# Row tiles of 32 for the first transforms, and filter taps of two terms with the products summed by VectorE in place

## The chip, the cores and the metric

The kernel runs on one NeuronCore of a Trainium2 chip. The core has a matrix engine (TensorE, PE in the profile, with its weight loads listed apart as PEld), VectorE (DVE), ScalarE (ACT), GpSimd (POOL) and a queue engine SyncE (SP) that here issues most of the transfers. The engines run side by side, each in its own fixed order, and wait for each other on semaphores. SBUF is the working memory of 128 partitions, PSUM the small memory into which TensorE writes its sums. The metric is the device time of one execution in microseconds, a median over executions; lower is better.

## The reference, cut to what matters

Two independent halves write the left and right 576 columns of a 2048 x 1152 output. The left half is a sliding window attention (32 heads of 18, window 256) behind a projection `x @ wqkv` and in front of `@ wo`. The right half is a state space convolution of `u` (2048 x 576) with a filter that is itself computed from 128 complex states for each channel:

```
P = jnp.exp(logdA[:, :, None] * l[None, None, :])
K = jnp.einsum("dn,dnl,dn->dl", Cc, P, dB).real      # the filter taps, d = 576, l = 2048
...
Yf = Uf * Kf                                         # FFTs over 2L = 4096
y  = irfft(Yf)[:L] + u * Dskip
```

So the filter taps K, the transforms of u and of K, their product and the inverse transform are what the right half computes. The kernel does the transforms by matrix products in two steps: a first transform of length 32 over the coarse index of time, a second of length 64 with the twiddles in its matrices.

## The kernel before, in words

The program has three stretches. The order of instructions in the first two is made by a planner: the instructions are traced in program order, and a scheduler places each on its engine by the costs that it assumes and by the dependences it sees; what the engine runs is that fixed order. The third stretch is placed in the written order (`manual_schedule`, line 991).

**Projection and tables, about 0 to 428 us.** Three generators are merged (lines 972 to 974): `proj` (lines 182 to 252, the projection, whose matmuls are on line 172 and whose results are read out by L236 on ScalarE and L237 on VectorE and stored by SP on L178 to L180 and L250), `tables` (lines 430 to 456, the filter), and `s1_u` (lines 470 to 477, the first transform of u).

The filter is built in 36 half groups c of 16 channels (`HC`); two halves form one of 18 groups. The 2048 taps of a channel are written as 32 coarse times 64 fine positions. For a half group:

- `exps_ab`, `exps_q`, `factors`, `phases` (lines 333 to 375 and 389 to 391) make small tables: outer products on TensorE (L314), exponentials and sines on ScalarE (L331), the fraction of an angle on ScalarE and VectorE (L324 to L326), and complex factors on GpSimd (L362 to L373). `factors` leaves A (12 wide: minus the imaginary part, the real part, the imaginary part) and `tr` (real and imaginary).
- `products` (lines 377 to 387) lets GpSimd multiply A with the real part of `tr` into m0 and A with the imaginary part into m1, each 128 partitions x 16 channels x 64 values in f32. Both come from pool P with two buffers for each name.
- `qtable` (lines 393 to 409) lets ScalarE make a sine and a cosine in PSUM and VectorE multiply them into Q (L404 to L407).
- `taps` (lines 411 to 428) is a sum over the states on TensorE in f32. For each channel four terms are accumulated in PSUM: both 32-wide halves of m0 and of m1, against the two halves of Q. Four channels at a time use four column strips of 32 of the array. After two half groups ScalarE copies kp into K (L428).

In `tables`, `taps(c - 1)` is written ahead of `products(c + 1)`: with two buffers the products of c + 1 reuse the buffers that the taps of c - 1 have read.

**The first transforms.** `s1` (lines 459 to 468) multiplies a block of 128 partitions (4 column groups of 144 channels x 32 coarse times) by a 128 x 128 matrix with four 32 x 32 blocks on its diagonal: one for the cosine part, one for the sine part. Each part goes through a PSUM bank (pool `pps`, three banks that the projection uses too), is copied out by ScalarE or every fourth time by VectorE (`evac`, L128 and L130) into a staging tile of pool `s1s` (two buffers), and is stored to DRAM by one transfer (L468). `s1_u` does this for u in 16 blocks during the first stretch; `s1_k` (lines 479 to 483) for K in 8 blocks after the last taps, with three PSUM banks of its own.

**Convolution and attention, from about 478 us.** `conv` (lines 485 to 585) loads for each of 16 pairs of frequencies the tables and the transformed u and K (`tx`, `tk`, L493 and L496, one pair ahead), transforms, multiplies, and inverts; it is woven into the attention by hand (lines 774 to 849).

What the change and the prediction touch: `w1` (lines 44 to 47 and 955), `gx` and `gk` (957, 958), the pools on 969 and 970, `products`, `taps`, `s1`, and `load` in `conv` (490 to 497).

Of the kernel before, what the change touches and what calls it, by code (L numbers as in the profile page):

```python
# [10 lines left out]
F32 = mybir.dt.float32  # L11
# [4 lines left out]
OP = mybir.AluOpType  # L16
# [10 lines left out]
JJ2 = JJ // 2  # L27
# [11 lines left out]
def constants():  # L39
    c = {}  # L40
    tau = 2 * np.pi
    l1, l2, f1, f2 = np.arange(32), np.arange(64), np.arange(32), np.arange(64)
    ph = -tau * np.outer(l1, f1 + 0.25) / 32
    w1 = np.zeros((128, 2, 128))
    for s in range(4):
        w1[s * 32:s * 32 + 32, 0, s * 32:s * 32 + 32] = np.cos(ph)
        w1[s * 32:s * 32 + 32, 1, s * 32:s * 32 + 32] = np.sin(ph)
    w2 = np.zeros((128, 32, 128))
    i1 = np.zeros((128, 32, 128))
    for f in range(32):  # L50
        ph = -tau * np.outer(l2, f + 0.25 + 32 * f2) / 2048
        co, si = np.cos(ph), np.sin(ph)
        w2[0:64, f, 0:64], w2[64:128, f, 0:64] = co, -si
        w2[0:64, f, 64:128], w2[64:128, f, 64:128] = si, co
        i1[0:64, f, 0:64], i1[64:128, f, 0:64] = co.T, si.T
        i1[0:64, f, 64:128], i1[64:128, f, 64:128] = -si.T, co.T
    ph = tau * np.outer(f1 + 0.25, l1) / 32
# [45 lines left out]
class Kernel:  # L103
# [271 lines left out]
        yield  # L375

    def products(self, c):
        A, tr = self.AB[c // 2]
        ch = slice(c % 2 * HC, c % 2 * HC + HC)
        sh = [128, HC, 8, 8]  # L380
        r = []
        for part, a0 in ((0, 4), (1, 0)):
            m = self.p["P"].tile(sh, F32, name="m%d" % part)
            self.nc.gpsimd.tensor_tensor(m, A[:, ch, a0:a0 + 8].unsqueeze(3).to_broadcast(sh),  # L384
                                         tr[:, ch, part, 0:8].unsqueeze(2).to_broadcast(sh), op=OP.mult)
            r.append(m.rearrange("p c a b -> p c (a b)"))
        self.P[c] = r

    def phases(self, c):
        x = self.outer(self.ps, c // 2, [self.mul["c_ct"]], c % 2 * HC, HC)  # L390
# [20 lines left out]
    def taps(self, c):  # L411
        nc = self.nc
        if c % 2 == 0:
            self.kp = self.p["kps"].tile([128, JJ, 64], F32, name="kp")
        kp, Q, (m1, m2) = self.kp, self.Q.pop(c), self.P.pop(c)
        for j in range(JJ2):
            for term in range(4):
                m = (m1, m2)[term // 2]
                a0 = term % 2 * 32
                for st in range(4):  # L420
                    ch = st * JJ2 + j
                    nc.tensor.matmul(kp[32 * st:32 * st + 32, c % 2 * JJ2 + j, :], m[:, ch, a0:a0 + 32],  # L422
                                     Q[:, ch, term % 2, :], start=(term == 0), stop=(term == 3), skip_group_check=True)
            if j % 2:
                yield
        if c % 2:
            q = c // 2
            nc.scalar.activation(self.K[:, :, q * JJ:q * JJ + JJ].rearrange("p l j -> p j l"), kp, AF.Copy)  # L428
# [28 lines left out]


    def s1(self, src, g, l0, nl, pp):
        nc, n = self.nc, nl * 144  # L460
        for part in range(2):
            st = self.p["s1s"].tile([128, n], F32, name="g1")
            k = n // 2 if n <= 576 else n // 3
            for o in range(0, n, k):
                ps = self.p[pp].tile([128, 512], F32, name="pp")[:, :k]
                nc.tensor.matmul(ps, self.w1[:, part, :], src[:, o:o + k], start=True, stop=True)  # L466
                self.evac(st[:, o:o + k], ps)
            nc.sync.dma_start(g[part, l0:l0 + nl].rearrange("l p j -> p l j"), st.rearrange("p (l j) -> p l j", j=144))  # L468

    def s1_u(self):  # L470
        uv = self.a["u"].rearrange("(p l) (s j) -> s p l j", l=64, j=144)
# [13 lines left out]
    def conv(self):  # L485
        nc, a, tt = self.nc, self.a, self.nc.vector.tensor_tensor
        fs, fy = self.p["fs"], self.p["fy"]

        def load(fp):
            t = {}  # L490
            for nm, src in (("w2", a["c_w2"]), ("i1", a["c_i1"])):
                t[nm] = fs.tile([128, 2, 128], F32, name=nm)
                nc.sync.dma_start(t[nm], src[:, 2 * fp:2 * fp + 2])  # L493
            for nm, g in (("tx", self.gx), ("tk", self.gk)):
                t[nm] = fs.tile([128, 4, 2, 144], F32, name=nm)
                nc.sync.dma_start(t[nm], g.rearrange("a l (s f) j -> (a l) s f j", s=4)[:, :, 2 * fp:2 * fp + 2, :])  # L496
            return t

        def ring():
# [69 lines left out]
        for qd in range(16):  # L569
# [7 lines left out]
            for hf in range(2):  # L577
                for k in range(2):
                    nc.tensor.matmul(pair[hf][64 * k:64 * k + 64], self.i2, hp[:, k, hf * 288:hf * 288 + 288],
                                     start=True, stop=True)  # L580
# [367 lines left out]
    def build(self):  # L948
        nc, a = self.nc, self.a
        with ExitStack() as es:  # L950
            self.pool(es, "const", 1)
            self.pool(es, "dram", 1, DRAM)
            self.pool(es, "dram2", 2, DRAM)
            cp, dp = self.p["const"], self.p["dram"]
            self.w1 = cp.tile([128, 2, 128], F32, name="w1")
            nc.gpsimd.dma_start(self.w1, a["c_w1"])
            self.gx = dp.tile([2, 64, 128, 144], F32, name="gx")
            self.gk = dp.tile([2, 64, 128, 144], F32, name="gk")
            self.h = dp.tile([2, 64, 32, D], F32, name="h")
            with ExitStack() as ek:  # L960
                self.pool(ek, "K", 1)
                with ExitStack() as e1:
                    for n, b, s in (("s4c", 1, None), ("pps", 3, PSUM), ("xps", 2, PSUM), ("trig", 1, PSUM),
                                    ("kps", 1, PSUM)):
                        self.pool(e1, n, b, s)
                    with ExitStack() as e2:
                        self.pool(e2, "prep", 1)
                        self.s4_prep()
                    for n, b in (("wq", 1), ("raw", 2), ("x", 1), ("pst", 2), ("s1u", 2), ("s1s", 2), ("ab", 2), ("abt", 1), ("mab", 4),
                                 ("mg", 4), ("fr", 2), ("Q", 2), ("P", 2)):  # L970
                        self.pool(e1, n, b)
                    proj, tables, s1u = self.proj(), self.tables(), self.s1_u()
                    merge((part(proj, 16), 16), (part(tables, 20), 20), (part(s1u, 4), 4))
                    merge((proj, 56), (tables, 304), (s1u, 12))
                with ExitStack() as e1:
                    self.pool(e1, "s1s", 2)
                    self.pool(e1, "s1p", 3, PSUM)
                    for _ in self.s1_k():
                        pass
            with ExitStack() as e1:  # L980
                self.pool(e1, "fc", 1)
                self.i2 = self.p["fc"].tile([128, 64], F32, name="i2")
                nc.sync.dma_start(self.i2, a["c_i2"])
# [44 lines left out]
```

## Time and profile before

| | |
|---|---|
| Median of 3 runs | 1046.06 us (1044.16 to 1049.4) |
| Profiled execution | 1041.77 us; its span from first to last instruction 1040.1 us |
| TensorE busy (matmuls) | 842.3 us, 81% of the span |
| VectorE busy | 703.1 us, 68% |
| ScalarE busy | 569.9 us, 55% |
| GpSimd busy | 593.5 us, 57% |
| First stretch, 104 to 416 us | TensorE busy 288.67 of 312 us |
| First transform of K, 430 to 478 us | transfers at 227 GB/s, DMA engines busy 76% |

A row of a group in the profile reads: line, engine, operation, output <- inputs by the program's names, shapes, count | busy time of the group and the mean duration of one in ns | idle time of the engine just before, with what ended it. The busy time is a union: where instructions overlap it is less than count times mean, and the ratio of the two says how many were in flight together. A row of a table by stretches gives the stretch, its length, then busy time and count for each engine, the granted TensorE clock as a share of full speed, the busy share of the DMA engines and GB/s. A row of waits gives the waiting engine, tile and line, what ended the wait, the total in us, how many times and the longest. A row of the chain gives start, length and what ran or was waited for. Each f32 matmul of the program appears as two TensorE instructions in the profile (the 64 matmuls that `taps` issues for a half group are its x128).

### The profile page before, as it was taken

The page shows a single profiled execution, that of the slowest core. Times are in us where ns is not written, and L with a number is a line of the kernel's source. Part 1 is how long each engine was busy: PE and PEld are TensorE (multiplying, and loading weights), DVE is VectorE, ACT ScalarE, POOL GpSimd, SP SyncE. Part 2 cuts the span into 40 slices and gives each one's busy share as a digit, 9 for nine tenths or more (in the row PEclk, how much of TensorE's full clock was granted, in tenths as well). Part 3 has the DMA queues.
Part 4 walks back from the last instruction along what each step waited for, and adds up shares of the span by engine and source line. Part 5 has one row for each costly group of instructions (what it writes and reads, how often), then busy time and mean ns, then how long its engine had stood idle before and what let it go on. Part 6 is the DMA issues. An engine that isn't in the chain of part 4 may idle for free.

```text
span 1040.1 us, 26776 instructions
## 1 busy us (share of the span) xinstructions
PE 842.3 (81%) x10332; PEld 443.0 (43%) x10332; DVE 703.1 (68%) x1805; ACT 569.9 (55%) x883; POOL 593.5 (57%) x714
## 2 busy tenths in 40 slices
PE   1433998989799899865788888878888999987787
PEld 0212456446457457532343333333333444433345
DVE  2879374674765675464867788878878676767554
ACT  1784466666666666331266565556666565634470
POOL 0036495674676596301266776757776757664780
PEclk9956899999999999898899999999999999989999
DMA  9655544443454333587144465464544563579863
GB/s 271 182 169 154 133 108 102 113 99 84 124 114 106 79 89 92 135 257 218 48 126 136 130 209 157 147 177 129 158 124 146 144 184 113 152 175 240 222 185 124
DMA packets 155911, 152.27 MB, mean 146 GB/s; under 512 B 36856, under 2 KB 134392, under 8 KB 155592
## 3 DMA queue, kind: packets, MB, share of 16 engines
q1 hardware_dynamic: 148152, 131.98, 46.8%
q0 software_dynamic: 6128, 14.60, 5.5%
q10 hardware_dynamic: 1504, 3.99, 1.4%
q8 instruction: 81, 1.33, 0.6%
q14 instruction: 46, 0.38, 0.1%
HBM read 89.12 MB, written 61.01 MB: 144 GB/s over the span
## 4 chain that ended last, share of the span: by engine, by line
PE 40%; DVE 21%; DMA 12%; issue 10%; ACT 7%; POOL 7%; SPq 2%; DVEq 0%; ACTq 0%; POOLq 0%
PE pp L172 11%; PE r L641 4%; PE kp L422 4%; PE r L505 4%; PE po L705 4%; PE r L908 4%; DVE jk L648 3%; PE pp L466 3%; POOL P L693 3%; PE x L314 2%; DMA gk<-g 2%; PE ST L682 2%; DVE qb L632 2%; ACT P L684 2%; PE r L513 2%
## 5 line engine op out<-in xcount | busy, mean ns | idle before, releaser
L648 DVE CUSTOM_DVE_ANT_0 jk<-r,bias 128x288 f32<-128x288 f32 (+7 forms) x512 | 198.4, 433 | 96.8 <-PE r L641 95.9
L684 ACT ACTIVATE P<-ST,esc 128x1024 f32<-128x1024 f32 (+1 forms) x192 | 201.8, 1058 | 94.5 <-PE ST L682 93.5
L693 POOL TENSOR_SCALAR_AFFINE_SELECT P<-P 128x512 f32<-128x512 f32 x240 | 171.1, 741 | 107.0 <-ACT P L684 104.6
L384 POOL TENSOR_TENSOR m<-A,tr 128x1024 f32<-128x1024 f32 x72 | 145.6, 2045 | 86.8 <-PE kp L422 79.6
L641 PE MATMUL r<-K,qb 128*64 128x288 f16 (+7 forms) x1024 | 130.4, 297 | 38.3 <-DVE qb L632 11.2
L541 POOL TENSOR_TENSOR Y<-t,t 64x288 f32<-64x288 f32 x64 | 52.9, 826 | 119.8 <-DMA tk<-gk 59.8
L705 PE MATMUL po<-P,V 128*32 128x256 f32 (+2 forms) x1408 | 100.6, 397 | 16.9 <-ACT osb L713 8.1
L641 PEld LDWEIGHTS <-qb 128*64 128x64 f16 x1024 | 60.1, 109 | 121.3 <-issue 67.3
L422 PE MATMUL kp<-Q,m 128*32 128x64 f32 x4608 | 80.6, 224 | 16.5 <-issue 6.1
L422 PEld LDWEIGHTS kp<-Q,m 128*32 128x32 f32 x4608 | 70.4, 112 | 38.8 <-issue 26.6
L466 PE MATMUL pp<-ut,w 128*128 128x288 f32 x128 | 47.8, 506 | 42.6 <-DMA ut<-in_u_dram 25.4
L682 PE MATMUL ST<-Q,K 64*128 64x384 f16 (+2 forms) x704 | 73.8, 281 | 3.0 <-DMA Q<-mt 2.9
L325 DVE TENSOR_TENSOR k<-x,k 128x512 f32<-128x512 f32 (+1 forms) x54 | 33.9, 638 | 39.1 <-ACT k L324 39.0
L237 DVE SCALAR_TENSOR_TENSOR qst<-pp,qst 128x512 f16<-128x512 f32 x36 | 24.7, 685 | 50.6 <-ACT qst L236 42.4
L705 PEld LDWEIGHTS po<-P,V 128*32 128x32 f32 x1408 | 35.8, 110 | 51.4 <-issue 26.4
L542 POOL TENSOR_TENSOR Y<-t,t 64x288 f32<-64x288 f32 x64 | 54.4, 851 | 3.8
L172 PE MATMUL pp<-xh,wh 128*128 128x512 f16 x180 | 48.3, 391 | 9.4 <-DVE xh L229 6.5
L128 ACT ACTIVATE g<-pp 128x288 f32<-128x288 f32 (+1 forms) x84 | 34.1, 447 | 37.9 <-DMA gk<-g 20.0
L362 POOL TENSOR_TENSOR tr<-tr,mab 128x768 f32<-128x768 f32 x18 | 34.7, 1929 | 31.1 <-ACT tr L331 31.1
L466 PEld LDWEIGHTS pp<-ut,w 128*128 128x128 f32 x128 | 26.5, 227 | 58.2 <-ACT g L128 17.5
L172 PEld LDWEIGHTS <-wh 128*128 128x128 f16 x324 | 31.6, 99 | 45.7 <-issue 12.4
L505 PE MATMUL r<-tx,w 128*64 128x288 f32 x256 | 41.2, 439 | 10.7 <-DMA tx<-gx 9.5
(173 smaller groups left out, 1755.4 us busy)
## 6 DMA issues: line engine op xcount, KB each, us to landing
gx<-g SPq DMA_DIRECT2D x32, 288.0 KB
qd<-qst SPq DMA_DIRECT2D x72, 128.0 KB
gk<-g SPq DMA_DIRECT2D x16, 576.0 KB
tx<-gx SPq DMA_DIRECT2D x16, 576.0 KB
tk<-gk SPq DMA_DIRECT2D x16, 576.0 KB
h<-ho SPq DMA_DIRECT2D x16, 576.0 KB
raw<-in_xT_dram SPq DMA_DIRECT2D x16, 512.0 KB
Q<-qd SPq DMA_DIRECT2D x32, 216.0 KB
```

The lines of the kernel that those rows point to most:

```text
L172: self.nc.tensor.matmul(ps, u, v, start=(i == 0), stop=(i == len(ops) - 1))
L384: self.nc.gpsimd.tensor_tensor(m, A[:, ch, a0:a0 + 8].unsqueeze(3).to_broadcast(sh), tr[:, ch, part, 0:8].unsqueeze(2).to_broadcast(sh), o ...
L422: nc.tensor.matmul(kp[32 * st:32 * st + 32, c % 2 * JJ2 + j, :], m[:, ch, a0:a0 + 32], Q[:, ch, term % 2, :], start=(term == 0), stop=(ter ...
L466: nc.tensor.matmul(ps, self.w1[:, part, :], src[:, o:o + k], start=True, stop=True)
L505: nc.tensor.matmul(ps[64 * par:64 * par + 64], w2[:, par, 64 * part:64 * part + 64], t[:, 2 * hs:2 * hs + 2, par, :], start=True, stop=True)
L542: nc.gpsimd.tensor_tensor(Y[par][64:128], t1[sl, 1], t2[sl, 1], op=OP.add)
L641: nc.tensor.matmul(ps[64 * b:64 * b + 64, :n], self.qb[:, b, t, :], d["K"][:, b, k0:k0 + n], start=True, stop=True, skip_group_check=True)
L648: nc.vector.tensor_tensor_reduce(out=jk[:, :n], in0=ps[:, :n], in1=self.bias[:, 288 - n:], scale=1.0, scalar=-3e38, op0=OP.add, op1=OP.max ...
L682: nc.tensor.matmul(ps[:, u, o:o + n], d["K"][h, jp, k0:k0 + 128], d["Q"][h, jp, q0:q0 + n], start=True, stop=True, skip_group_check=True)
L684: nc.scalar.activation(pt[:, 2 * jp:2 * jp + 2, lo:hi], ps[:, :, lo:hi], AF.Exp, scale=self.esc)
L693: nc.gpsimd.affine_select(v, v, pattern=[[0, 4], [sg, 128]], compare_op=OP.is_ge, fill=0.0, base=-1 if far else 0, channel_multiplier=-sg)
L705: nc.tensor.matmul(self.po[32 * j:32 * j + 32, t0 * 128:t1 * 128], V[:, kb * 76 + 19 * j:kb * 76 + 19 * j + 32], pt[:, j, o:o + (t1 - t0) ...
```

## The change

- The matrix of the first transform becomes one 128 x 64 tile: 32 rows of cosine next to sine, repeated for the four groups of 32 partitions. `s1` issues for each piece of columns four matmuls with 32 rows and 64 columns of weights, one for each group of partitions, into the lower and upper halves of two PSUM tiles allocated together, in place of two matmuls with 128 rows and 128 columns. The number of read-outs stays. The staging tiles get two names (g0, g1) with two buffers each. Each block is stored by four transfers of 64 partitions in place of two of 128; the elements of 576 bytes stay.
- `gx` and `gk` in DRAM become [64, 4, 64, 144], and `load` fetches `tx` and `tk` by two transfers of 64 partitions each in place of one of 128.
- In `products`, VectorE adds m1 to m0 in place after GpSimd has made both. `taps` accumulates two terms in place of four. Pool P becomes P0 with two buffers for m0 and P1 with one buffer for m1.

```diff
-        w1[s * 32:s * 32 + 32, 0, s * 32:s * 32 + 32] = np.cos(ph)
-        w1[s * 32:s * 32 + 32, 1, s * 32:s * 32 + 32] = np.sin(ph)
+    w1 = np.tile(np.concatenate([np.cos(ph), np.sin(ph)], axis=1), (4, 1))
...
-            m = self.p["P"].tile(sh, F32, name="m%d" % part)
+            m = self.p["P%d" % part].tile(sh, F32, name="m%d" % part)
...
-            r.append(m.rearrange("p c a b -> p c (a b)"))
-        self.P[c] = r
+            r.append(m)
+        self.nc.vector.tensor_tensor(r[0], r[0], r[1], op=OP.add)
+        self.P[c] = r[0].rearrange("p c a b -> p c (a b)")
...
-            for term in range(4):
-                m = (m1, m2)[term // 2]
-                a0 = term % 2 * 32
+            for term in range(2):
                 for st in range(4):
                     ch = st * JJ2 + j
-                    nc.tensor.matmul(kp[32 * st:32 * st + 32, c % 2 * JJ2 + j, :], m[:, ch, a0:a0 + 32],
-                                     Q[:, ch, term % 2, :], start=(term == 0), stop=(term == 3), skip_group_check=True)
+                    nc.tensor.matmul(kp[32 * st:32 * st + 32, c % 2 * JJ2 + j, :], P[:, ch, 32 * term:32 * term + 32],
+                                     Q[:, ch, term, :], start=(term == 0), stop=(term == 1), skip_group_check=True)
...
     def s1(self, src, g, l0, nl, pp):
         nc, n = self.nc, nl * 144
-        for part in range(2):
-            st = self.p["s1s"].tile([128, n], F32, name="g1")
-            k = n // 2 if n <= 576 else n // 3
-            for o in range(0, n, k):
-                ps = self.p[pp].tile([128, 512], F32, name="pp")[:, :k]
-                nc.tensor.matmul(ps, self.w1[:, part, :], src[:, o:o + k], start=True, stop=True)
-                self.evac(st[:, o:o + k], ps)
-            nc.sync.dma_start(g[part, l0:l0 + nl].rearrange("l p j -> p l j"), st.rearrange("p (l j) -> p l j", j=144))
+        st = [self.p["s1s"].tile([128, n], F32, name="g%d" % e) for e in range(2)]
+        k = n // 2 if n <= 576 else n // 3
+        for o in range(0, n, k):
+            ps = [self.p[pp].tile([128, 512], F32, name="pp")[:, :k] for _ in range(2)]
+            for q in range(4):
+                r, h = slice(32 * q, 32 * q + 32), 64 * (q % 2)
+                nc.tensor.matmul(ps[q // 2][h:h + 64], self.w1[r], src[r, o:o + k], start=True, stop=True,
+                                 skip_group_check=True)
+            for e in range(2):
+                self.evac(st[e][:, o:o + k], ps[e])
+        for q in range(4):
+            h = 64 * (q % 2)
+            nc.sync.dma_start(g[l0:l0 + nl, q].rearrange("l p j -> p l j"),
+                              st[q // 2][h:h + 64].rearrange("p (l j) -> p l j", j=144))
...
-                nc.sync.dma_start(t[nm], g.rearrange("a l (s f) j -> (a l) s f j", s=4)[:, :, 2 * fp:2 * fp + 2, :])
+                for e in range(2):
+                    f0 = 32 * e + 2 * fp
+                    nc.sync.dma_start(t[nm][64 * e:64 * e + 64], g[:, :, f0:f0 + 2])
...
-            self.w1 = cp.tile([128, 2, 128], F32, name="w1")
+            self.w1 = cp.tile([128, 64], F32, name="w1")
...
-            self.gx = dp.tile([2, 64, 128, 144], F32, name="gx")
-            self.gk = dp.tile([2, 64, 128, 144], F32, name="gk")
+            self.gx = dp.tile([64, 4, 64, 144], F32, name="gx")
+            self.gk = dp.tile([64, 4, 64, 144], F32, name="gk")
...
-                                 ("mg", 4), ("fr", 2), ("Q", 2), ("P", 2)):
+                                 ("mg", 4), ("fr", 2), ("Q", 2), ("P0", 2), ("P1", 1)):
```

More of the change, by code (lines that the diff above doesn't have):

```diff
@@ L43, in constants @@
     ph = -tau * np.outer(l1, f1 + 0.25) / 32
-    w1 = np.zeros((128, 2, 128))
-    for s in range(4):
-        w1[s * 32:s * 32 + 32, 0, s * 32:s * 32 + 32] = np.cos(ph)
-        w1[s * 32:s * 32 + 32, 1, s * 32:s * 32 + 32] = np.sin(ph)
+    w1 = np.tile(np.concatenate([np.cos(ph), np.sin(ph)], axis=1), (4, 1))
     w2 = np.zeros((128, 32, 128))
@@ L414, in taps @@
             self.kp = self.p["kps"].tile([128, JJ, 64], F32, name="kp")
-        kp, Q, (m1, m2) = self.kp, self.Q.pop(c), self.P.pop(c)
+        kp, Q, P = self.kp, self.Q.pop(c), self.P.pop(c)
         for j in range(JJ2):
-            for term in range(4):
-                m = (m1, m2)[term // 2]
-                a0 = term % 2 * 32
+            for term in range(2):
                 for st in range(4):
                     ch = st * JJ2 + j
-                    nc.tensor.matmul(kp[32 * st:32 * st + 32, c % 2 * JJ2 + j, :], m[:, ch, a0:a0 + 32],
-                                     Q[:, ch, term % 2, :], start=(term == 0), stop=(term == 3), skip_group_check=True)
+                    nc.tensor.matmul(kp[32 * st:32 * st + 32, c % 2 * JJ2 + j, :], P[:, ch, 32 * term:32 * term + 32],
+                                     Q[:, ch, term, :], start=(term == 0), stop=(term == 1), skip_group_check=True)
             if j % 2:
```

## The prediction

> **What bounds the kernel now.** I read the busy shares of 40 slices first: TensorE is near full only from the fifth to the sixteenth slice, so I asked for the stretch in which the changed code runs, then for its chain, its waits and its groups. First the busy times by stretch (TensorE, weight loads, VectorE, ScalarE, GpSimd; clock, DMA share, GB/s):
>
> ```profile
> 104.00:416.00 312.00, 288.67 (x5147) 176.32 (x5150) 188.26 (x278) 196.98 (x351) 203.61 (x161) 0.98 0.44 104
> 416.00:430.00 14.00, 10.10 (x381) 8.56 (x371) 6.46 (x10) 4.17 (x7) 9.12 (x8) 0.89 0.45 102
> 430.00:478.00 48.00, 35.87 (x96) 17.40 (x94) 28.57 (x27) 16.13 (x36) 0.40 (x1) 0.96 0.76 227
> ```
>
> From 104 to 416 us TensorE is busy 92.5% of the time and no other engine over 66%: it is the bound there. From 430 to 478 us, the first transform of K, nothing is full but the transfers come nearest. The chain of that stage (start, length, what):
>
> ```profile
> 434.26 3.43 DMA gk<-g
> 437.79 0.50 ACT g L128
> 438.33 2.22 PE pp L466 x6
> 440.57 0.57 DVE g L130
> 441.20 5.37 DMA gk<-g
> ```
>
> It is a loop over two staging buffers: store, wait until it has landed, read out into the freed buffer, store. Next the waits of VectorE and GpSimd from 104 to 416 us:
>
> ```profile
> POOL m L384 <- PE kp L422: 79.0, 9, 14.1
> POOL tr L362 <- ACT tr L331: 21.4, 12, 4.0
> ...
> DVE qst L237 <- ACT qst L236: 42.4, 17, 5.5
> DVE k L325 <- ACT k L324: 39.0, 11, 14.2
> DVE Q L406 <- ACT sn L331: 16.6, 12, 2.7
> ```
>
> GpSimd makes products as soon as the taps free a buffer, and VectorE never waits for GpSimd. Groups with count, union and mean, from the page:
>
> ```profile
> L384 POOL TENSOR_TENSOR m<-A,tr 128x1024 f32<-128x1024 f32 x72 | 145.6, 2045 | 86.8 <-PE kp L422 79.6 <-issue 7.2
> L422 PE MATMUL kp<-Q,m 128*32 128x64 f32 x4608 | 80.6, 224 | 16.5 <-issue 6.1
> L466 PE MATMUL pp<-ut,w 128*128 128x288 f32 x128 | 47.8, 506 | 42.6 <-DMA ut<-in_u_dram 25.4
> L682 PE MATMUL ST<-Q,K 64*128 64x384 f16 (+2 forms) x704 | 73.8, 281 | 3.0 <-DMA Q<-mt 2.9
> L505 PE MATMUL r<-tx,w 128*64 128x288 f32 x256 | 41.2, 439 | 10.7 <-DMA tx<-gx 9.5
> ```
>
> Count times mean over union gives the matmuls in flight: 1.36 in L466 on the whole array, 2.7 in L505 on two column halves, 2.7 in L682 on two row halves, 12.8 in L422 on four column strips. Last, VectorE beside GpSimd (start, length):
>
> ```profile
> 301.96 1.78 DVE L326 TENSOR_SCALAR ab<-k 128x512 int32<-128x512 int32 x1
> ```
>
> This operation takes 0.34 us at best and 2.15 at worst. Here GpSimd ran products from 299.57 us, 1.99 each; the second ended near 303.55 and L326 at 303.74. The two engines exclude each other in such cases.
>
> **The change, part by part.** The sum is made against the profiled execution, 1041.77 us, span 1040.1 us; the median of the three runs is 4.3 us above it.
>
> *Taps of two terms.* Half of L422's instructions go. From 104 to 416 us they hold TensorE 67.85 us, so 33.9 us go, all on the bounding engine.
>
> *Row tiles for u.* In that stretch L466 holds TensorE 27.0 us (x88, 11 of the 16 blocks). The new form has twice the instructions, each with a quarter of the rows and half of the columns of the array. No row shows f32 in row tiles. If four run together (as four strips do in L422), 13.5 us go; if only two do (L505, L682), nothing; if none, 27 us are added. L682 shows row tiles overlapping and L422 four in flight, so I take four. TensorE needs 288.7 - 33.9 - 13.5 = 241.3 us.
>
> *The sums on VectorE.* 36 additions of 128 x 1024 f32, both inputs in SBUF. Nearest rows with two SBUF inputs: 512 elements 0.68 us at best (L764), 576 elements 0.76 us (L575). At about 1.04 ns an element plus 0.15 us one takes 1.21 us, 33 of them (65 products lie in this stretch) 40 us. L764's median is 1.12 and its longest 1.29 us, in the stretch where GpSimd works beside it. So each addition may also wait out a product that GpSimd has begun: 0 to 1.95 us; I take half, 1 us, since GpSimd pauses after many products (the 79 us of waits). VectorE: 188.3 + 40 + 33 = 261 us. GpSimd, held during the additions: 203.6 + 40 = 244 us at most.
> The Trainium skill, "SBUF — State Buffer", section "SBUF: two separate sides", says it more strongly: the pair of ports that the two engines share is an exclusive lock for a whole instruction, and a VectorE operation with two SBUF inputs takes it. L326 agrees (1.78 for 0.34 us). By that rule every addition right behind a product whose successor has started would pay the full 1.95 us.
>
> *What bounds that stretch then.* Three engines at 241 to 261 us, ScalarE at 197. With the 92.5% that TensorE reaches now the largest gives 282 us; with 90%, because three nearly equal engines wait for each other more often, 290. I take 286: 26 us less than 312. Ends: 261 us (TensorE alone bounds, additions never wait) and 316 us (all additions pay 1.95 us: 188.3 + 40 + 64 = 292 at 92.5%), that is -51 to +4. The planner will lay out a new order, which no row shows.
>
> *The new wait.* An addition at the head of VectorE's queue until its m1 is there holds back the read-outs of the projection (L237), the fractions and Q. Behind them stand TensorE (PSUM banks) and ScalarE's sines. With one buffer for m1 the next m1 waits for the addition too. In the order of before the products lay several us ahead of their taps, so I charge nothing beyond the 1 us above and make the rest a rival.
>
> *78 to 104 us.* Here VectorE is busy 23.91 of 26 us and carries the chain; two additions fall in: +2.4 us.
>
> *416 to 430 us.* The last taps run alone, L422 busy 6.1 us: half goes, -3 us (0 to -6, with the 2.5 us in which TensorE waited for its instructions).
>
> *First transform of K.* TensorE has 35.87 us in 48 and is not the bound; the buffers are, 27.3 us of read-outs waiting for `gk<-g` to land. With twice the staging the stage runs at what the transfers give: 227 GB/s x 48 us = 10.9 MB; at the 257 GB/s of its best slice 42.4 us, at the kernel's best slice (271) 40.2. I take -5.5 us (-8 to 0, should stores of 64 partitions be slower).
> The skill's page just named, section "Door 1: The DMA port swizzle", gives 64 partitions half of 436 GB/s, 218; if the halves did not overlap, 9.44 MB of stores would take 43 us, and the gain would be nearer 4 us. No row here shows it.
>
> *SP.* 22 more issues of gx at 0.38 us by 416 us, 16 more of gk, 64 more for tx and tk of at most 0.6 us. Behind them on SP stand the stores of qd; SP's waits from 104 to 416 us sum to over 140 us, which hides 9 us. The loads of tx and tk are issued a pair of frequencies ahead, and TensorE waited for tx once (9.5 us, at the start): +0.5 us there. If that cover went, each pair would pay some 0.6 us, 10 in all.
>
> Sum: -26 + 2.4 - 3 - 5.5 + 0.5 = -31.6, so 1010 for the profiled execution and 1014 against the median.
>
> **The rivals.**
> - *VectorE stands for GpSimd (slower).* The planner places the addition where the real product, at 2 us, is not done. If each waits one product and half of another, 2.9 us: (188.3 + 33 x 4.1) / 0.925 = 350 us, +38. With the other terms 1074, against the median 1079. It decides above 2.1 us a wait, where the stage grows by the 5.6 us that the other terms gain and another 5. For it: GpSimd's products start late now, behind the taps, and VectorE's order is fixed. Against it: three PSUM banks of projection work (3 us each) lie between VectorE and TensorE.
> - *VectorE becomes the bound with full waits for the ports.* Stage +4, sum -1.6: 1044, no change. For it L326; against it GpSimd's pauses.
> - *The row tiles do not overlap.* TensorE 288.7 - 33.9 + 27 = 282, at 92.5% 305 us, -7; the K stage has 72 us of matmul in place of 36, +24. Sum +17: 1063. Against it L682.
> - *TensorE stays the only bound.* -51 + 2.4 - 6 - 8 = -62.6: 984. For it: every wait of VectorE in the stretch follows TensorE's or ScalarE's work.
>
> **How the numbers follow.** Forecast 1014, chance 0.50, its own range 996 to 1034 (the stage at 94% or 85% of the largest demand, 278 to 307). TensorE alone 984: 0.14. No change 1044: 0.14. VectorE standing 1079: 0.15. Row tiles serial 1063: 0.07. Half a per cent, 5 us, is about what a measurement tells from no change. Faster: 0.50 + 0.14 + a third of the 1044 case = 0.69. Same: 0.10. Slower: 0.21. The range leaves out half of the fastest case and most of the slowest: 986 to 1062.
>
> **What would show it.** Right: L422 x2304 with half the busy time; the stretch from 104 us to the last taps about 25 us shorter; TensorE below 90% in it; the new addition near 1.2 to 2.2 us; L466 with twice the count and about half the union; hardly a wait for `gk<-g`. Wrong: long waits of VectorE for m on line 384's successor, then of ScalarE and TensorE for VectorE; L466 with a larger union; landing times of gk above 5.4 us.

## The result and the profile after

The changed kernel takes 1104.83 us in the median (1098.41 to 1110.41) against 1045.11 us for the kernel before on the same chip: 1.056 times as long, 95% interval 1.049 to 1.064. Its profiled execution took 1098.41 us, the span is 1096.7 us against 1040.1. Five marks, each the start of an instruction that both kernels have, say where the 56.6 us lie:

| mark, us from the span's start | before | after | stretch ending there |
|---|---|---|---|
| first matmul of the projection | 105.8 | 118.7 | +12.9 |
| last read-out of kp into K | 428.4 | 465.0 | +23.7 |
| last store of gk issued | 476.7 | 505.0 | -8.3 |
| first matmul on tx | 484.4 | 537.4 | +24.7 |
| end of the span | 1040.1 | 1096.7 | +3.6 |

So the filter's stretch lost 36.6 us in two pieces, the transform of K gained 8.3, and then 24.7 us were lost in a place that holds no changed instruction but the loads of tx and tk. The same three stretches as busy times of the changed kernel (TensorE, weight loads, VectorE, ScalarE, GpSimd; clock, DMA share, GB/s):

```profile
118.70:465.01 346.31, 295.80 (x3377) 153.92 (x3376) 234.66 (x318) 200.71 (x358) 213.52 (x166) 0.90 0.42 96
468.00:505.00 37.00, 28.38 (x180) 9.15 (x176) 6.69 (x12) 15.41 (x34) 0.00 (x0) 0.87 0.89 232
506.00:537.00 31.00, 0.00 (x0) 0.00 (x0) 21.67 (x16) 0.00 (x0) 3.51 (x1) 0.50 0.52 131
```

In the first row TensorE is busy 85% and VectorE 68%: nobody is full, yet the stretch is longer. The same stretch of the kernel before, from its own first projection matmul to its last read-out into K:

```profile
105.79:428.41 322.62, 298.26 (x5512) 184.37 (x5511) 191.96 (x285) 198.33 (x355) 211.14 (x168) 0.98 0.44 104
```

TensorE's busy time is 296 us in place of 298 although 39% of its instructions are gone: the granted clock is 0.90 against 0.98, and one and the same group of projection matmuls takes 440 ns in the mean against 391. In the last row of the three TensorE and ScalarE do nothing at all for 31 us while VectorE and GpSimd fill memory. The groups of the changed kernel that answer to those shown before:

```profile
L382 POOL TENSOR_TENSOR m<-A,tr 128x1024 f32<-128x1024 f32 x72 | 144.9, 2023 | 94.0 <-PE kp L419 54.0
L465 PE MATMUL pp<-ut,w 32*64 32x288 f32 x256 | 50.5, 545 | 44.9 <-DMA ut<-in_u_dram 24.3
L385 DVE TENSOR_TENSOR m<-m,m 128x1024 f32<-128x1024 f32 x36 | 48.1, 1338 | 53.2 <-POOL m L382 52.9
L419 PE MATMUL kp<-Q,m 128*32 128x64 f32 x2304 | 54.3, 239 | 26.2 <-DVE Q L406 9.8
```

L385 is the new sum: 1.34 us in the mean, less than the 2.2 us costed with the wait for the ports, but VectorE stood 52.9 us in front of it for GpSimd's product. L419 has half the instructions and two thirds of the time of L422, not half. L465, the row tiles, has 256 x 0.545 / 50.5 = 2.8 matmuls in flight against 1.36, and twice as many to do: no gain. The waits of the changed kernel from 104 to 468 us:

```profile
POOL m L382 <- PE kp L419: 54.0, 9, 9.3
PEld L169 <- issue: 50.5, 99, 4.0
DVE m L385 <- POOL m L382: 48.5, 18, 7.8
POOL m L382 <- DVE m L385: 38.5, 25, 2.8
...
ACT sn L328 <- DVE Q L406: 28.6, 10, 7.2
...
PE x L311 <- DVE k L322: 20.2, 11, 3.7
```

The two engines that did not wait for each other before now do so both ways, and TensorE's weight loads for the projection (L169) wait 50.5 us for nothing that the profile names, against 21.9 before. The taps hardly wait for the sum itself (0.8 us, once). What comes late is VectorE's other work: TensorE waits 20.2 us for the fractions (L322), against 3.4 before, and ScalarE 28.6 us for Q, against 20.9. The first of the two pieces begins ahead of the projection; from the same kernel in order of time (start, length):

```profile
83.10 2.96 DVE L385 TENSOR_TENSOR m<-m,m 128x1024 f32<-128x1024 f32 x1 [4.46 <-POOL m L382]
...
86.25 4.15 DVE L207 SCALAR_TENSOR_TENSOR wl<-K,wr,wh 128x2160 f16<-128x2160 f32 x1
...
118.70 4.96 PE L169 MATMUL pp<-xh,wh 128*128 128x512 f16 x12 [0.66 <-ACT xh L223]
```

VectorE stands 4.5 us for the first product with the splitting of the weights (L207) queued behind, which the projection needs; the sum and the split each take longer beside GpSimd (2.96 and 4.15 us against 1.21 and 2.46 at best). This is not the whole 12.9 us: with the sums alone (e3 below) VectorE stands 6.1 us at the same place, and the projection starts only 2 us later. Last, the empty stretch behind the transform of K:

```profile
509.57 3.51 POOL L603 MEMSET qb<- 128x4096 f16 x1 [47.87 <-DMA i<-in_c_i_dram]
509.65 0.30 DVE L599 MEMSET bias<- 128x288 f32 x1 [6.40 <-DMA i<-in_c_i_dram]
...
530.02 1.21 SPq L502 DMA_DIRECT2D tx<-gx  x2
...
537.42 2.19 PE L511 MATMUL r<-tx,w 128*64 128x288 f32 x8 [34.77 <-DMA tx<-gx]
```

These are the attention's set-up: memsets, and loads that SP issues in turn with them. Before, the same memsets ran from 427 to 475 us beside the transform of K. Now they start some 4.5 us after its last store was issued, and the loads of tx stand behind them on SP. The profile names a load (`i`) as what released them here; e1 has the same gap, and there it names a store of gk.

### The profile page after: what moved, and what is told of

Same layout as the page of the kernel before. It is cut to its first block, busy times and chain, and to the rows that moved or that the text cites. A ratio compares the mean times of both kernels' runs of the same rounds, so it can differ in the third digit from the quotient of the medians.

```text
span 1096.7 us, 22681 instructions
## 1 busy us (share of the span) xinstructions
PE 839.6 (77%) x8252; PEld 400.8 (37%) x8252; DVE 751.1 (68%) x1841; ACT 570.3 (52%) x883; POOL 599.5 (55%) x714
## 4 chain that ended last, share of the span: by engine, by line
PE 19%; DVE 13%; issue 6%; POOL 5%; DMA 4%; ACT 2%; SPq 1%; DVEq 0%; POOLq 0%; ACTq 0%
PE r L647 4%; PE po L711 4%; PE r L511 4%; DVE jk L654 3%; PE r L914 3%; POOL P L699 2%; PE ST L688 2%; PE r L519 2%; DVE qb L638 2%; DVE osb L770 1%; DMA out_dram<-t 1%; ACT P L690 1%; DMA X<-in_u_dram 1%; DVE m L654 1%; DVE t L542 1%
## 5 line engine op out<-in xcount | busy, mean ns | idle before, releaser
L465 PE MATMUL pp<-ut,w 32*64 32x288 f32 x256 | 50.5, 545 | 44.9 <-DMA ut<-in_u_dram 24.3
L385 DVE TENSOR_TENSOR m<-m,m 128x1024 f32<-128x1024 f32 x36 | 48.1, 1338 | 53.2 <-POOL m L382 52.9
L419 PE MATMUL kp<-Q,m 128*32 128x64 f32 x2304 | 54.3, 239 | 26.2 <-DVE Q L406 9.8
L359 POOL TENSOR_TENSOR tr<-tr,mab 128x768 f32<-128x768 f32 x18 | 38.6, 2146 | 54.0 <-ACT tr L328 47.4
L169 PE MATMUL pp<-xh,wh 128*128 128x512 f16 x180 | 56.7, 440 | 10.2 <-DVE xh L226 8.2
L419 PEld LDWEIGHTS kp<-Q,m 128*32 128x32 f32 x2304 | 41.6, 120 | 55.7 <-issue 26.3
L537 ACT ACTIVATE X<-r 128x288 f32<-128x288 f32 x64 | 25.6, 410 | 65.7 <-DMA tk<-gk 36.8
L169 PEld LDWEIGHTS <-wh 128*128 128x128 f16 x324 | 33.1, 105 | 56.2 <-issue 27.4
L169 PE MATMUL pp<-xh,wl 128*128 128x512 f16 x180 | 50.9, 410 | 0.0
L328 ACT ACTIVATE mg<-x 128x512 f32<-128x512 f32 x72 | 40.7, 599 | 13.2 <-PE x L311 12.8
```

The source lines that it names most:

```text
L169: self.nc.tensor.matmul(ps, u, v, start=(i == 0), stop=(i == len(ops) - 1))
```

## The experiments

Ratios are against runs of the kernel before beside them on the same chip (medians 1042 to 1044 us), with the 95% interval.

### The staging of K's transform

**e1, four staging buffers in the kernel before, nothing else.**

```diff
-                    self.pool(e1, "s1s", 2)
+                    self.pool(e1, "s1s", 4)
```

> The kernel before with one edit: four staging buffers in place of two for the first transform of K alone. Theory L (layout): doubling that staging, as the change does by its two names, makes it reach the addresses of the attention's set-up tiles, so that the set-up (memsets of VectorE and the loads of the first units, about 20 us) can start only when the last store of K's transform has landed. Then: the stage some 5 to 7 us shorter, the stretch from its last store to the first matmul on tx some 25 us longer, in all 1060 to 1068 against 1045. Rival S (stores): the late set-up comes from the four stores of 64 partitions, which are not here. Then 1038 to 1045.

1058.77 us, 1.0145 (1.0104 to 1.0186), just below the range of theory L. The two stretches of this kernel, and the start of the set-up:

```profile
436.00:462.00 26.00, 26.00 (x82) 15.30 (x81) 5.58 (x10) 14.88 (x31) 0.00 (x0) 1.00 1.01 288
465.00:496.00 31.00, 0.00 (x0) 0.00 (x0) 20.74 (x16) 0.00 (x0) 3.51 (x1) 0.57 0.50 142
```

```profile
470.52 0.30 DVE L593 MEMSET bias<- 128x288 f32 x1 [5.15 <-DMA gk<-g]
```

The stage falls from 48.3 to 34.6 us, at 288 GB/s in the stretch shown, more than expected, and the same empty 31 us appear behind it. No store of 64 partitions is in this kernel, so theory L holds and S falls. In the profiled execution another 8 us lie behind the first matmul on tx (3.6 in the changed kernel); what they are was not looked into.

**e2, the changed kernel with one buffer for each staging name.**

```diff
-                    self.pool(e1, "s1s", 2)
+                    self.pool(e1, "s1s", 1)
```

> The changed kernel with one edit: one staging buffer for each of the two names in the first transform of K, so as many bytes as in the kernel before. Theory L: the set-up goes back beside the stage, which loses its 7 us: 1080 to 1090 against 1105. Rival S: the late set-up stays, 1105 to 1112.

1098.11 us, 1.0527 (1.0483 to 1.0571), against 1.0564 for the change. The set-up is back beside the stage (first matmul on tx 11.4 us behind the last store, against 32.4), as theory L has it. But the time is a miss for it: the stage grew from 40 to 66 us. Its waits:

```profile
PEld pp L465 <- ACT g L125: 41.1, 20, 5.0
ACT g L125 <- DMA gk<-g: 32.8, 10, 6.7
...
DVE g L127 <- DMA gk<-g: 19.7, 3, 7.4
```

With one buffer each, both tiles are filled side by side and stored together, and the next block stands until they have landed. The kernel before fills and stores its two in turn.

**e11, three buffers in the kernel before.**

```diff
-                    self.pool(e1, "s1s", 2)
+                    self.pool(e1, "s1s", 3)
```

> The kernel before with three staging buffers in place of two in the transform of K, which by theory L still fit beside the attention's tiles. The set-up stays beside the stage, and the stage gains some of the 14 us that four buffers gave it: 1036 to 1043 against 1044. If any growth of that staging moves the set-up behind the stage: 1055 to 1062.

1041.42 us, 0.9978 (0.9953 to 1.0002): no clear difference. In its profile the stage takes 41.6 us in place of 48.3, the set-up stays beside it (first matmul on tx 11.5 us after the last store). So the set-up moves between three and four buffers. The sizes in the program fit: K takes 36,864 bytes of a partition and each buffer 4,608; the three pools opened ahead of the attention's take 2,560 + 31,744 + 18,432 = 52,736. Three buffers end at 50,688, four at 55,296, 2,560 bytes inside the set-up's first tiles. The changed kernel has four.

### The two halves of the change

**e3, sums and taps of two terms alone** (`products`, `taps` and the pools P0 and P1 of the change in the kernel before).

> The kernel before with the second half of the change alone: products summed by VectorE, taps of two terms, pools P0 and P1; the first transforms as before. Theory V (VectorE stands for GpSimd's products, and TensorE, less busy, runs at a lower granted clock): the stretch to the last taps 30 to 40 us longer, VectorE waiting 40 to 60 us for m, 1075 to 1085 in all. Rival R (the row tiles, their four stores and the pairs of banks are what lengthens the first stretch): 1015 to 1040.

1067.91 us, 1.0237 (1.0196 to 1.0277). The last read-out into K comes at 458.6 us against 428.4, and all of the loss lies ahead of it. Its waits from 104 to 440 us:

```profile
DVE m L388 <- POOL m L385: 42.2, 18, 7.6
POOL m L385 <- DVE m L388: 37.2, 25, 2.8
```

The place is as theory V has it; the time lies below its 1075 to 1085.

**e4, row tiles, four stores and the new layout alone**, with one buffer for each staging name in both stretches.

> The kernel before with the first half of the change alone: row tiles, four stores, new layout of gx and gk; taps and products as before; staging of one buffer for each of the two names in both stretches, as many bytes as before. Theory V and L: nothing in the first stretch depends on it, TensorE gains little, 1035 to 1050. Rival R: the first stretch 20 to 40 us longer, 1065 to 1085.

1069.38 us, 1.0237 (1.0195 to 1.0278): the rows cost as much as the sums. The time lies in rival R's range, but not for its reason: the last read-out into K is 9.8 us later than before, not 20 to 40, and the transform of K takes 64.8 us in place of 48.3, which no theory here had.

**e10, the same with two stores of 128 partitions** (the new layout allows them).

```diff
-        for q in range(4):
-            h = 64 * (q % 2)
-            nc.sync.dma_start(g[l0:l0 + nl, q].rearrange("l p j -> p l j"),
-                              st[q // 2][h:h + 64].rearrange("p (l j) -> p l j", j=144))
+        for e in range(2):
+            nc.sync.dma_start(g[l0:l0 + nl, 2 * e:2 * e + 2].rearrange("l q p j -> (q p) l j"),
+                              st[e].rearrange("p (l j) -> p l j", j=144))
```

> The row tiles alone with two stores of 128 partitions for each block in place of four of 64; nothing else differs from the run with the rows alone (1069). Theory S (the four stores, 0.6 us of SP each against 0.37, and their slower landing, cost the time): the first stretch 5 to 10 us shorter, the transform of K 5 to 12 us shorter, 1048 to 1060. Rival P (both staging tiles are filled and stored together, so that read-outs and stores no longer take turns; and TensorE falls to half its granted clock): 1063 to 1070.

1059.49 us, 1.0148 (1.0102 to 1.0194). The four stores account for about 10 us, nearly all in the transform of K, which falls to 55.7 us. The first stretch gains 1.4 us, not theory S's 5 to 10.

**e15, the pairing without the rows**: both banks of a piece filled together by matmuls of 128 rows, both staging tiles filled side by side, one buffer each, two stores.

> The kernel before with the order of the row version and without its row tiles: both PSUM banks of a piece filled together, the two staging tiles filled side by side and stored by two transfers of 128 partitions, one buffer each; matmuls of 128 rows as before. If this pairing with one buffer each is what remains of the cost of the rows (1059 with two stores): 1053 to 1062. If the row tiles themselves are: 1040 to 1049.

1054.67 us, 1.0116 (1.0077 to 1.0156). Most of what was left with two stores is the pairing; the row tiles and the new layout are worth the rest, 0.3%, with intervals that overlap. By place, in the profiled executions: the pairing costs in the transform of K, 54.2 us here against 48.3 before and 55.7 in e10. The later read-out into K is not in e15 (428.9 us, against 436.8 in e10 and 428.4 before), so it goes with the row tiles or the layout. Beside each other, the transform of K in e10 and in e15:

```profile
440.00:497.00 57.00, 41.29 (x184) 13.02 (x180) 28.67 (x27) 15.76 (x36) 0.00 (x0) 0.53 0.66 197
```

```profile
436.00:485.00 49.00, 34.74 (x85) 15.54 (x83) 28.11 (x26) 14.47 (x32) 0.00 (x0) 0.93 0.72 214
```

TensorE is busy 72% and 71% of these stretches, but the row tiles run at a granted clock of 0.53 and the full matmuls at 0.93.

### What the sum costs

**e5, taps of two terms without the sum** (m1 is made and left out of the taps).

```diff
-        self.nc.vector.tensor_tensor(r[0], r[0], r[1], op=OP.add)
```

> Taps of two terms without the sum: GpSimd makes both products as before, VectorE adds nothing, TensorE reads m0 alone (the share of m1 in the filter is left out). It shows what halving the taps is worth on TensorE alone. Theory V (the sum and its waits cost the time, the halved taps would save it): the stretch to the last taps 20 to 35 us shorter than before, 1008 to 1025 in all. Rival C (TensorE's time is not what bounds the stretch: with less to do it waits more, and runs at a lower granted clock): within 10 us of before, 1032 to 1050.

1018.83 us, 0.975 (0.9711 to 0.9789). The last read-out into K comes at 408.3 us, 20 earlier than before. So TensorE was the bound of this stretch, and halving the taps pays when nothing is asked for it. The taps of e5 need not wait for m1 either, but that gives nothing: they waited 7.5 us in all for a product, against 4.5 before.

**e6, 36 sums on zeros of VectorE's own**, m1 left out.

```diff
-        self.nc.vector.tensor_tensor(r[0], r[0], r[1], op=OP.add)
+        self.nc.vector.tensor_tensor(self.scr, self.scr, self.scr, op=OP.add)
```

> As the run without the sum, but VectorE makes 36 additions of the same size and with two SBUF inputs on a tile of zeros of its own, which wait for nothing of GpSimd (the share of m1 is left out of the filter). The work of the sum without its wait. Theory V with the wait as the cost: close to the run without the sum, at most 15 us above it. Rival W (the work and the ports are the cost): near the run with taps alone, 1058 to 1070.

1037.04 us, 0.992 (0.9885 to 0.9956), between the two. It does not settle the question: as the sums waited for nothing, the planner had all of them done by 175 us, 17 of the 36 ahead of 104 us.

**e16, the same work spread**: each sum reads the Q that VectorE has just made.

```diff
+        v = Q[:, 0:HC // 2].rearrange("p c t m -> p (c t m)")
+        nc.vector.tensor_tensor(self.scr, self.scr, v, op=OP.add)
         self.Q[c] = Q
```

> As the run without the sum, with 36 additions of the same size on VectorE, two SBUF inputs each, but each on a tile of its own and the first half of the Q that VectorE has just made: spread over the half groups as the sums are, and waiting for nothing of GpSimd (the share of m1 is left out of the filter). Run e6 had them all done by 175 us, so it did not settle this. If the waits for GpSimd's products are most of the cost: 1026 to 1040. If VectorE's work and the exclusion of the two engines are: 1052 to 1068.

1042.97 us, 1.0017 (0.9986 to 1.0049), again between the two ranges. The sums ran from 93 to 427 us, 1.46 us each in the median. First e5, then e16, then e3, each from near the first projection matmul to about the last read-out into K:

```profile
109.90:408.30 298.40, 270.35 (x3289) 153.31 (x3288) 196.62 (x284) 198.28 (x357) 209.35 (x165) 0.96 0.46 109
```

```profile
105.00:428.00 323.00, 278.28 (x3318) 156.37 (x3322) 257.74 (x332) 202.76 (x362) 228.22 (x166) 0.94 0.43 102
```

```profile
107.80:458.60 350.80, 296.34 (x3386) 163.82 (x3385) 245.27 (x329) 205.31 (x366) 216.63 (x168) 0.89 0.40 95
```

The last read-outs come at 408.3, 429.3 and 458.6 us. The work of the sums, spread and waiting for nobody, takes back the 20 us that the halved taps gave (+21); with the wait for GpSimd it takes 29 more. VectorE is busy longer in e16 than in e3 and the stretch still ends earlier: the difference is not VectorE's work.

The granted clock has a share in it. TensorE's busy time times its granted clock, an estimate of its work at full clock from these rows, is 292 us before, 260 in e5, 262 in e16, 264 in e3 and 266 in the changed kernel. So the halved taps saved 26 to 33 us of work in all four. What differs is that TensorE stands idle for longer (28 us in e5, 45 in e16, 54 in e3) and that the same work takes longer at a lower clock (270, 278, 296 us busy). In these rows the clock is lower where TensorE is busy for a smaller share; whether the waiting lowers the clock was not tested, and neither was the planner's order, which differs between the three.

**e7, the sum one half group later**, at the head of `taps(c)`, with two buffers for m1.

```diff
-        self.nc.vector.tensor_tensor(r[0], r[0], r[1], op=OP.add)
-        self.P[c] = r[0].rearrange("p c a b -> p c (a b)")
+        self.P[c] = r
...
-        kp, Q, P = self.kp, self.Q.pop(c), self.P.pop(c)
+        kp, Q, r = self.kp, self.Q.pop(c), self.P.pop(c)
+        nc.vector.tensor_tensor(r[0], r[0], r[1], op=OP.add)
+        P = r[0].rearrange("p c a b -> p c (a b)")
```

> Taps of two terms with the sum written at the head of taps(c) in place of the end of products(c), that is one half group later, and two buffers for m1: the same work, the same result, but the planner may put it behind more of VectorE's other work. Theory V: VectorE's waits for m fall from 42 us to under 15, 1030 to 1050 against 1068 with taps alone. Rival W: 1058 to 1070.

1053.48 us, 1.0091 (1.006 to 1.0121): 14 us better than e3, between the two ranges. The waits did not fall below 15 us but to this:

```profile
DVE m L417 <- POOL m L385: 35.2, 15, 6.8
```

**e8, two buffers for m1**, the sum where the change has it (`("P1", 2)`).

> Taps alone with two buffers for m1 in place of one, the sum where the change has it. GpSimd's 37 us of waits for the sum should go. Theory V: they cost little, since it is VectorE's standing that counts: 1060 to 1070 against 1068. Rival B (the single buffer is what lengthens the stretch): 1035 to 1050.

1064.9 us, 1.0193 (1.0155 to 1.0231), 3 us better than e3 in the median, with intervals that overlap. The single buffer matters little, and VectorE stands longer than in e3:

```profile
DVE m L388 <- POOL m L385: 60.4, 23, 7.2
```

**e9, the sum on GpSimd.**

```diff
-        self.nc.vector.tensor_tensor(r[0], r[0], r[1], op=OP.add)
+        self.nc.gpsimd.tensor_tensor(r[0], r[0], r[1], op=OP.add)
```

> Taps alone with the sum on GpSimd, behind its own two products, so that VectorE waits for nothing of GpSimd. GpSimd gets 36 sums of about 2 us more (211 to some 285 us in a stretch of about 320). Theory V: the waits of VectorE for m go to none, and the time falls from 1068 to 1022 to 1045, between the run without the sum (1019) and that with the work elsewhere (1037) unless GpSimd becomes the bound. Rival G (GpSimd is the new bound, TensorE waits for m): 1050 to 1065.

1049.94 us, 1.005 (1.0025 to 1.0075): 18 us better than on VectorE, though a sum there takes 2.36 us in the median. That is the edge of rival G, and its mechanism: GpSimd is busy 284 of 329 us, and now TensorE waits for it:

```profile
PEld kp L422 <- POOL m L388: 21.5, 8, 5.4
...
PE kp L422 <- POOL m L388: 17.9, 6, 5.3
```

**e12, the same with three staging buffers.**

> The sum on GpSimd and three staging buffers together. Their gains lie in different stretches and should add: 4 to 8 us below the run with the sum on GpSimd alone.

1050.73 us, 1.0063 (1.0037 to 1.0088), a miss: the gains did not add. The last store of gk comes 8 us earlier, but the first matmul on tx only 2 (490.1 against 492.3).

**e13 and e14, the sum for every second half group from the sixth on (16 of 36)**, on GpSimd with three staging buffers, and on VectorE with two; four terms for the others.

```diff
-        self.nc.vector.tensor_tensor(r[0], r[0], r[1], op=OP.add)
-        self.P[c] = r[0].rearrange("p c a b -> p c (a b)")
+        if c % 2 and c > 4:
+            self.nc.gpsimd.tensor_tensor(r[0], r[0], r[1], op=OP.add)      # e14: nc.vector
+            r = r[:1]
+        self.P[c] = [m.rearrange("p c a b -> p c (a b)") for m in r]
```

> Half of the change's first idea: the sum on GpSimd for every second half group from the sixth on (16 of 36), four terms for the others, two buffers for each product, and three staging buffers in the transform of K. TensorE saves 16 x 0.96 = 15 us, GpSimd gets 16 x 2.4 = 38 us and stays under 80% of the stretch. If GpSimd at 86% was what held the run with all sums there, TensorE is the bound again and the time falls to 1025 to 1035. If any wait of the taps for a sum costs as much as it saves: 1038 to 1048.

> The same 16 sums on VectorE at the change's place, staging of K's transform as before. If the cost of VectorE's standing grows with the number of sums and each costs more than the taps save (25 us for 36 sums), 16 of them give +8 to +14: 1051 to 1058. If the cost comes from the crowd of all 36 (three engines near their limits at once), half as many leave slack and it is 1030 to 1043.

e13: 1043.87 us, 0.9998 (0.9981 to 1.0015), no difference, as if each wait cost what the taps save. e14: 1073.0 us, 1.0267 (1.0233 to 1.0301), a miss on both sides: 16 sums on VectorE, with two buffers for each product, cost no less than 36 (1.0237 in e3; the intervals overlap). The crowd of all 36 is not the reason then. From the waits of e14 from 104 to 460 us:

```profile
DVE m L389 <- POOL m L385: 31.3, 13, 4.1
```

13 of 16 sums were waited for, 2.4 us each, about double of what the taps of such a half group save (33.9 us over some 31 half groups, 1.1 us each). Why so few cost so much stays open; the order that the planner lays out is new in each of these kernels. No version tried that computes the whole filter beats the kernel before clearly.

## Why the prediction was wrong, step by step

The forecast of 1014 us was wrong in direction. Three steps of its sum failed: the stretch up to the last taps was put at -29 us (-26 and -3) and came to +23.7, because it was taken as the largest busy demand at a fixed use; within it the new wait was put at nothing; and the first loads of tx were put at +0.5 us and came to +24.7. Term by term:

- **Taps of two terms**: 33.9 us less on TensorE was right as a price at the clock of before: busy time times granted clock fell by some 33 us (292 to 260 in e5). The busy time itself fell by 28 us in e5 and by 2 in the changed kernel. Without the sum the last read-out came 20 us earlier (e5); that TensorE was the bound, the reading everything else rested on, held.
- **The sums on VectorE**: 1.21 us for the instruction was right, 1.23 in the median. The 1 us for the ports was too much: the mean is 1.34 us, 0.13 above the shortest, and 30 of the 36 took 1.21 to 1.23 us. The nearest reading is that VectorE often stands at a sum when GpSimd's product ends (19 times), before GpSimd has begun the next, so that the full 1.95 us that the Trainium skill's page "SBUF — State Buffer" (section "SBUF: two separate sides") would charge behind a started product was rarely paid. Two sums did take long, 2.81 and 2.96 us, as if they had waited out most of a product.
- **What bounds that stretch then** is the first step that failed. It took the longest of three demands at 90 to 92.5% of use. VectorE's demand of 235 us was lower than the 261 forecast; TensorE's, put at 241, was 296 at the lower clock; and no engine was over 85%. Before, TensorE bounded the stretch while GpSimd waited 79.0 us for it. With a sum between GpSimd and TensorE, VectorE waits for GpSimd (48.5 us), GpSimd for the sums (38.5) and for the taps (54.0), and TensorE and ScalarE wait for what stands behind the sum in VectorE's queue. e16 shows that the work alone took the gain; e3, with the waits and at the lower clock that came with them, lost as much again and more. How much of that is the clock stays open.
- **The new wait** is the second: "I charge nothing beyond the 1 us" was wrong by some 29 us (e3 against e16, the clock included). The products did lie several us ahead of their taps, but the sum does not stand where the taps stand. It stands ahead of VectorE's read-outs and fractions, where the planner puts it. The rival of VectorE standing for GpSimd had the right mechanism, but not the right formula: e3 waited 42 us in all, some 1.3 us for each sum, below the 2.1 us from which it was to decide. With 1.3 us a wait its formula gives a stage of some 293 us, shorter than before.
- **78 to 104 us**: +2.4 forecast. The projection started 12.9 us later in the changed kernel, but 2 with the sums alone and 4.4 with the rows alone. The two do not add up to it; the rest stays open.
- **Row tiles for u**: -13.5 forecast, with "nothing" as the other end; the other end it was. Their union is 50.5 us against 47.8, with 2.8 matmuls in flight, like the two halves (2.7) that were to give nothing.
- **First transform of K**: -5.5 forecast, -8.3 measured, near in size, but in part by luck. The doubled staging alone does help (three buffers take 6.7 us off in e11), but the sign "hardly a wait for `gk<-g`" did not come: 24.6 us of read-outs still waited for it, against 27.3. The memsets also left this stage, where they had filled VectorE between the read-outs; what that gave was not separated. The Trainium skill's page "SBUF — State Buffer" (section "Door 1: The DMA port swizzle") gives 218 GB/s for 64 partitions; that would be the rate here if the halves did not overlap. The trace shows more, 245 GB/s from 470 to 505 us, and 288 in e1 with stores of 128.
- **"+0.5 there"** for the first loads of tx is the third step that failed: 24.7 us. The price of the extra issues was fine; what went wrong was to look only at what the change adds to SP. The doubled staging was counted as a gain, and the prediction did not ask which later tiles lie on those bytes (e1, e2, e11).
- **SP**: with one buffer for each name the four stores cost about 10 us (e10 against e4), not hidden: in the transform of K the read-outs waited 49.8 us for `gk<-g` in e4 and 23.9 in e10. A store of 64 partitions takes SP 0.57 us or more against 0.36. What the four stores cost with the change's two buffers was not tried.

## What to carry to other kernels

A step that removes work from the bounding engine by giving another one a wait must be costed as a ring: who waits for whom, and what stands behind the waiter in its queue; here busy time with room to spare said nothing of it. Staging that grows is memory taken from whatever is allocated there next, and work that was hidden beside a stage can fall out behind it by a few kilobytes. Leave the new work out once (e5), and put it in once without its wait (e16): the two runs give prices that no profile of the kernel before holds, each for the order that the planner lays out for it.

## What the runs showed of the hardware that was not expected

- The same share of TensorE's time got very different clocks: 0.53 with matmuls of 32 rows and 64 columns (e10, and 0.53 in e2 and e4), 0.93 with full ones (e15), both busy 71 to 72%. In the changed kernel, with deeper staging, the row tiles had 0.87 at 77% busy. The lower clock itself lengthens the busy time (a row-tile matmul on K took 0.84 us in the median in e10 and 0.53 in the changed kernel), so equal shares are not equal work. That the rows are the reason is a reading that was not tested by itself.
- Four matmuls of a quarter of the rows and half the columns did not run four at a time: eight instructions for a piece of 384 columns took 1.24 us in a run of their own, where four full ones took some 1.45 (2.22 us for six in the kernel before). The four write into two PSUM tiles, two into each; whether that is the reason was not tried.
- Issuing a store of 64 partitions kept SP longer (0.57 us at least; 0.63 in the median in e4 with the DMA engines 62% busy, 1.07 in the changed kernel with 89%) than one of 128 with twice the bytes (0.36 in the median, in e1 with 91% too).
